# The second half of the last layer down as seven block products over pairs of token tiles

## The chip, the core and the metric

The kernel runs on one core of a Trainium2 chip. The metric is the device time of one execution, in microseconds (us); less is better.

## What is computed

Three stages follow each other: a decayed linear attention, a gated layer pair, and a second layer pair with three branches of which the largest counts. All is float32. The change is in the last line.

```python
# q, k, v: (2, 8, 768, 64), lam: (8,); per block of 64 positions
intra = (q_b @ k_b.T * lam ** (i - j) for i >= j) @ v_b
inter = (q_b * lam ** (i + 1)) @ kv_state
kv_state = lam ** 64 * kv_state + (k_b * lam ** (63 - i)).T @ v_b
x = (intra + inter) as (1536 tokens, 512)
x = ((x @ w_a) * (x @ w_b)) @ w_out                # 512 -> 1536 -> 512
h = max(x @ w1, x @ w2, x @ w3)                    # 512 -> 768
out = h @ w_out                                    # 768 -> 512: the last layer down
```

## The kernel before

**Products in three.** TensorE multiplies a rounded form of float32 (`F32R` in the code). Every operand is split into a high part, a ScalarE copy to that form, and a low part, a VectorE subtraction of the high part from the whole (`split_part`, L525). Each product is then three matmuls: high x high, low x high, high x low.

**Layers up.** All but two column groups of the layers up use Winograd's form of Strassen's product: a 2 x 2 block product in seven block products (`PROD`) with sums of operand blocks before (S1 to S4, T1 to T4) and sums of results after. `Group.product` (L591) issues six matmuls of 384 columns for each; `largest` (L655) adds the results up and keeps the maximum of the three branches in six tiles `m0` to `m5` of 128 features x 1536 tokens each (`ha` in the code). Their first 768 columns are the first half of the tokens.

**The last layer down.** `down2` (L775) multiplies the tokens, 12 tiles of 128, with the 768 x 512 weights; tokens are the stationary operand and the weights stream through. The first half, tiles 0 to 5, goes feature group by feature group (k = 0 to 5) into six PSUM banks, `out0` to `out5`, all open at once: 108 matmuls of 512 columns. The first two of its 36 steps are issued among the last products of the layer up. At k = 5 each tile's bank is copied to SBUF by ScalarE (`ob`) and sent out by a DMA of SP's queue (`store`, L752). The second half, tiles 6 to 11, goes tile by tile: 18 matmuls of 512 columns each, the last tile in two halves of 256 columns, whose last copy is VectorE's (L761). PSUM has eight banks of 512 columns.

**Weights.** They come in as 64-bit numbers and are put together by `converted` (L211): VectorE shifts (L221), ScalarE scales (L224), VectorE merges twice (L229, L231). `down_block` (L310) does this for blocks of 768 columns and splits them: four blocks for the last layer, put in pairs in `dh`, `dl` (k = 0 to 2) and `hd`, `ld` (k = 3 to 5).

**Order.** Each engine has a queue of its own and takes it in the order in which it was written. A planner (`Pace`) writes the work of VectorE and ScalarE between the matmuls: a task is a generator whose steps are written as soon as its gates are open and its engine is estimated to have room (`pump`), or at the latest when somebody needs the result (`need`). The splits of `m0` to `m5` are such tasks, for either half of the tokens (`finished2`, L1021). SBUF work tiles come from a ring of 26 slots of 1536 columns (`slot`), the PSUM banks from a ring of eight (`bank`).

Of the kernel before, what the change touches and what calls it, by code (L numbers as in the profile page):

```python
# [11 lines left out]
F32R = mybir.dt.float32r  # L12
AF = mybir.ActivationFunctionType
ALU = mybir.AluOpType

B, H, S, D = 2, 8, 768, 64
# [3 lines left out]
NT = B * S  # L20
# [5 lines left out]
K2 = F2 // 128  # L26
J = 384
TT = 512
NTT = NT // TT
WB = 768  # L30
ND1 = K1 * DM // WB
ND2 = K2 * DM // WB
N1 = K1
N2 = 3 * K2 // 2
# [9 lines left out]
PROD = {  # L44
    1: ("A11", "B11", "z"), 6: ("S2", "T2", "z"), 7: ("S3", "T3", "z"), 4: ("A22", "T4", "z"),
    2: ("A12", "B21", "x"), 5: ("S1", "T1", "b"), 3: ("S4", "B22", "b"),
}
FIRST = (1, 2, 5)
# [115 lines left out]
def decay_attention_gated_mlps(ctx: ExitStack, tc: tile.TileContext, qkv: bass.AP, lam: bass.AP, wup: bass.AP, wdown: bass.AP, out: bass.AP):  # L164
    nc = tc.nc
# [6 lines left out]
    pace = Pace()  # L172

    def slot(name, dt=F32):
        return sp.tile([128, 1536], dt, tag="s", name=name)

    def zt(name):
        return zp.tile([128, J], F32, tag="z", name=name)

    def bank(name):  # L180
        return pp.tile([128, 512], F32, tag="ps", name=name)

    def rd(t):
        return t.bitcast(F32)

    def tt(e, o, a, b, op):
        (nc.vector if e == "DVE" else nc.gpsimd).tensor_tensor(out=o, in0=a, in1=b, op=op)  # L187

    def copy(o, a):
        nc.scalar.activation(out=o, in_=a, func=AF.Copy)  # L190
# [4 lines left out]
    at_item = {x: n for n, x in enumerate(items)}  # L195
# [110 lines left out]
        tt(e, t7[:, 6], t7[:, 2], t7[:, 0], ALU.subtract)  # L306

    dparts, dunit = {}, {}

    def down_block(m, i):  # L310
        roomy = 1 <= i < ND1 - 1 or i == ND1 + 3
        yield "gate", ("done", m - (2 if roomy or i == ND1 + 1 else 1))
        yield "gate", ("conv", m)
        t = yield from converted(m, WB, roomy)
        yield "gate", ("split", m)
        if i in (0, ND1 + 2):
            dparts[i // 2] = [hp.tile([128, 1536], F32R, tag="h", name=f"{x}{i}", padded_shape=[128, 1792]) for x in ("hd", "ld")]
        elif i % 2 == 0:
            dparts[i // 2] = slot(f"dh{i}", F32R), slot(f"dl{i}", F32R)
        hi, lo = dparts[i // 2]  # L320
        s = slice(WB * (i % 2), WB * (i % 2) + WB)
        yield ("ACT",), WB, "S"
        copy(hi[:, s], t[:, 0:WB])
        e = yield EITHER, WB, "S"
        tt(e, lo[:, s], t[:, 0:WB], rd(hi[:, s]), ALU.subtract)
        pace.open(("done", m))
        for k in range(3):
            if k // 2 <= i % 2 and (i // 2, k) not in dunit and (k == 0 or i % 2):
                dunit[i // 2, k] = hi[:, 512 * k:512 * k + 512], lo[:, 512 * k:512 * k + 512]

# [20 lines left out]

    def unit(first, k):
        b = first // 2 + k // 3
        m = at_item["down", first + (3 * (k // 3) * 512 // WB) + (0 if k % 3 == 0 else 1)]
        items_to(m)
        pace.need(wtask[m], lambda: (b, k % 3) in dunit)
        return dunit[b, k % 3]
# [167 lines left out]
    def split_part(a, h, l):  # L525
        n = a.free_size()
        yield ("ACT",), n, "S"
        copy(h, a)
        e = yield EITHER, n, "S"
        tt(e, l, a, rd(h), ALU.subtract)  # L530

    class Operands:
# [6 lines left out]
        def __init__(self, a, name, order=ORDER, given={}):  # L539
            self.ops, self.name, self.given = dict(given), name, given  # L540
            plain = order is not self.ORDER
            for x in given:
                pace.open((name, "part", x))
            a11, a12, a21, a22 = a[0][:, 0:2], a[0][:, 2:4], a[1][:, 0:2], a[1][:, 2:4]
            s12 = slot(f"{name}s12").rearrange("p (s a n) -> p s a n", s=2, a=2)
            s1, s2 = s12[:, 0], s12[:, 1]
            self.sums = {"S1": (s1, a21, a22, ALU.add), "S2": (s2, s1, a11, ALU.subtract), "S3": (a21, a21, a11, ALU.subtract), "S4": (s1, a12, s2, ALU.subtract)}
            self.src = {"A11": a11, "S1": s1, "S2": s2, "A12": a12, "A21": a21, "S3": a21, "A22": a22, "S4": s1}
            self.tasks = {}
            for i, x in enumerate(order):  # L550
                t = self.tasks[x] = pace.add(self.make(i if not plain else x, x, plain), 0.7 if plain and x[0] == "S" else 0)
                for g in ("sum", "part"):
                    pace.opens[name, g, x] = t
# [30 lines left out]
    class Group:  # L584
# [6 lines left out]
        def product(self, p):  # L591
            a, b, where = PROD[p]
            if p in FIRST:
                self.bank[where] = bank(f"{where}{self.name}")
            ps = self.bank[where][:, 0:J]
            wh, wl = weights(self.n, b)
            xh, xl = self.ops(self.j).get(a)
            todo = [(w[:, 128 * k:128 * k + 128], x[:, k]) for k in range(2) for w, x in ((wh, xh), (wh, xl), (wl, xh))]
            for i, (w, x) in enumerate(todo):
                nc.tensor.matmul(ps, w, x, start=p in FIRST and i == 0, stop=i == len(todo) - 1, skip_group_check=p not in FIRST)  # L600
            pace.pe(6 * MM, self.free.get(where, 0.0))
            if p in (1, 6, 7):
                z = self.z[p] = zt(f"z{p}{self.name}")
                copy(z, ps)
                self.free["z"] = pace.run("ACT", J)
            self.done(self, p, ps)
# [28 lines left out]
    def tokens(j, b):  # L635
        return slice((2 * j + b) * J, (2 * j + b) * J + J)
# [16 lines left out]
    ha = {}  # L653
# [98 lines left out]
    def store(i, c, cols, ps, vector=False):  # L752

        j, b, r = i // 6, i // 3 % 2, i % 3
        row = b * S + j * J + 128 * r
        s = slice(c, c + cols)
        if c == 0:
            store.ob = slot(f"ob{i}")
        ob = store.ob
        if vector:  # L760
            nc.vector.tensor_copy(ob[:, s], ps)  # L761
        else:
            copy(ob[:, s], ps)
            pace.run("ACT", cols)
        nc.sync.dma_start(out=out[row:row + 128, s], in_=ob[:, s])

    def down2_part(i, k, ps, s):
        o = tokens(i // 6, i // 3 % 2).start + 128 * (i % 3)
        (ah, al), (wh, wl) = hs[k], unit(ND1, k)
        pace.need(htask[k, i // 6])  # L770
        for n, (a, w) in enumerate(((ah, wh), (al, wh), (ah, wl))):
            nc.tensor.matmul(ps, a[:, o:o + 128], w[:, s], start=k == 0 and n == 0, stop=k == K2 - 1 and n == 2)  # L772
        pace.pe(3 * MM5 * (s.stop - s.start) / 512)

    def down2():  # L775

        n = NT // 128
        ps = {}
        for k in range(K2):
            for i in range(6):  # L780
                if k == 0:
                    ps[i] = bank(f"out{i}")
                down2_part(i, k, ps[i], slice(0, 512))
                if k == K2 - 1:
                    store(i, 0, 512, ps[i])
                yield
        for i in range(6, n):
            last = i == n - 1
            cols = 256 if last else 512
            for c in range(0, 512, cols):  # L790
                p = bank(f"out{i}_{c}")[:, c:c + cols]
                for k in range(K2):
                    down2_part(i, k, p, slice(c, c + cols))
                store(i, c, cols, p, last and c > 0)

    with tc.manual_schedule():
        nc.sync.dma_start(out=lams, in_=lam)
# [218 lines left out]
            pace.open(("y0", i))  # L1016
            pace.open(("y1", i))
        yo[1] = Operands([ya[1, b] for b in range(B)], "y1")
        hs, htask = {}, {}

        def finished2(at, g):  # L1021
            n = g.n - N1
            f, i = divmod(n, 3)
            if g.j == 1:
                for d in (n + 2, n + 3):
                    if d < N2:
                        open_to("conv", base + d)
                if n + 2 < N2:
                    open_to("split", base + n + 2)
                for d in {N2 - 3: (0,), N2 - 2: (1,), N2 - 1: (2, 3)}.get(n, ()):  # L1030
                    open_to("conv", base + N2 + d)
                    open_to("split", base + N2 + d)
            if i == 2:
                for k in (f, f + K2 // 2):
                    if g.j == 0:
                        hs[k] = slot(f"hh{k}", F32R), slot(f"hl{k}", F32R)
                    s = slice(768 * g.j, 768 * g.j + 768)
                    htask[k, g.j] = pace.add(split_part(ha[k][:, s], hs[k][0][:, s], hs[k][1][:, s]), 2)

        def each2(at, g):  # L1040
            f, i = divmod(g.n - N1, 3)
# [7 lines left out]
        for i, _ in enumerate(in_slots(groups, each2, finished2)):  # L1049
            if 7 * len(groups) - i in (3, 2):  # L1050
                next(then)
        for _ in then:
            pass

# [50 lines left out]
```

## Time and profile before

| | |
|---|---|
| median of 3 runs | 508.27 us (508.13 to 508.62) |
| the profiled execution | 508.21 us |
| its span from first to last instruction | 506.5 us |
| TensorE matmuls, busy | 499.0 us (99%) |
| VectorE, busy | 376.9 us (74%) |
| ScalarE, busy | 213.6 us (42%) |
| GpSimd, busy | 57.7 us (11%) |

Busy time is the time in which an engine has an instruction under way. Matmuls overlap in the records, so their distance, not their length, tells how fast TensorE goes. PE is TensorE's matmul, PEld its weight load, DVE VectorE, ACT ScalarE, POOL GpSimd, SP the engine whose queue issues the DMAs.

### The profile page before, as it was taken

How to read it: one execution, taken by the hardware profiler on the slowest of the kernel's cores; microseconds unless marked ns; L12 is line 12 of the kernel's file. 1: busy time of each engine (PE TensorE's matmuls, PEld its weight loads, DVE VectorE, ACT ScalarE, POOL GpSimd, SP SyncE). 2: the span in 40 equal slices, each digit the busy share in tenths (PEclk: the TensorE clock that was granted, in tenths of full speed). 3: DMA queues.
4: the chain of work that ended last, by engine and by line, in shares of the span. 5: the costliest groups of instructions: out<-in, count | busy, mean ns of one | idle time of the engine just before them, and what ended most of it. 6: DMA issues, size and time to landing. Idle time of an engine off the chain costs nothing.

```text
span 506.5 us, 7757 instructions
## 1 busy us (share of the span) xinstructions
PE 499.0 (99%) x3163; PEld 466.2 (92%) x3163; DVE 376.9 (74%) x559; ACT 213.6 (42%) x360; POOL 57.7 (11%) x50
## 2 busy tenths in 40 slices
PE   7899999999999999999999999999999999999997
PEld 6799899999999999997888888899999999998886
DVE  6899878787788777789685089679998999897000
ACT  2434445343344443445542455543554454433211
POOL 4685200211111011211000000000000000000000
PEclk9999999999999999999999999999999999999999
DMA  8996002222222101314331021102211111110311
GB/s 295 412 410 257 2 1 84 83 84 83 84 83 85 59 11 58 125 63 129 142 107 60 0 83 32 54 1 83 84 60 47 63 62 63 63 63 0 126 62 63
DMA packets 10404, 47.17 MB, mean 93 GB/s; under 512 B 1280, under 2 KB 1536, under 8 KB 7808
## 3 DMA queue, kind: packets, MB, share of 16 engines
q1 hardware_dynamic: 10368, 46.67, 25.1%
q8 instruction: 25, 0.41, 0.3%
q14 instruction: 11, 0.09, 0.1%
HBM read 43.52 MB, written 3.15 MB: 92 GB/s over the span
## 4 chain that ended last, share of the span: by engine, by line
PE 94%; DVE 4%; DMA 1%; issue 0%; ACT 0%; SPq 0%; DVEq 0%
PE yp L718 18%; PE zu L600 16%; PE zv L600 15%; PE out L772 10%; PE bu L600 8%; PE bv L600 7%; PE p L619 7%; PE xu L600 4%; PE xv L600 4%; PE s L416 2%; PE o L472 1%; DVE am L423 1%; PE k L485 1%; PE o L459 1%; DMA aq<-qkv_dram 1%; DVE gl L187 1%
## 5 line engine op out<-in xcount | busy, mean ns | idle before, releaser
L187 DVE TENSOR_TENSOR lo<-w,hi 128x1024 fp32r<-128x1024 f32 (+2 forms) x41 | 48.2, 1175 | 12.4 <-ACT hi L190 12.4
L190 ACT ACTIVATE hi<-w 128x1024 fp32r<-128x1024 f32 (+2 forms) x41 | 38.5, 938 | 22.7 <-DVE w L262 6.9
L718 PE MATMUL yp<-gh,dh 128*128 128x512 f32 x108 | 42.0, 389 | 0.0
L718 PE MATMUL yp<-gl,dh 128*128 128x512 f32 x108 | 42.0, 389 | 0.0
L718 PE MATMUL yp<-gh,dl 128*128 128x512 f32 x108 | 42.0, 389 | 0.0
L650 POOL TENSOR_TENSOR g<-z1u,z6u 128x384 f32<-128x384 f32 x20 | 24.0, 1199 | 149.9 <-DVE z6u L632 149.9
L187 DVE TENSOR_TENSOR gl<-g,gh 128x512 fp32r<-128x512 f32 x36 | 24.7, 707 | 17.8 <-ACT gh L190 17.8
L187 DVE TENSOR_TENSOR w<-w 128x256 f32<-128x256 f32 (+1 forms) x57 | 30.9, 541 | 1.0
L761 DVE COPY ob<-out 128x256 f32<-128x256 f32 x1 | 0.4, 425 | 38.4 <-PE out L772 38.4
L229 DVE SCALAR_TENSOR_TENSOR w<-ws,w 128x1024 int32<-128x1024 int32 x20 | 26.0, 1300 | 1.1 <-ACT ws L224 1.1
L231 DVE SCALAR_TENSOR_TENSOR w<-ws,w 128x1024 int32<-128x1024 int32 x20 | 25.8, 1288 | 0.3
L190 ACT ACTIVATE z6u<-zu 128x384 f32<-128x384 f32 x20 | 9.8, 492 | 38.2 <-PE zu L600 38.1
L190 ACT ACTIVATE z7u<-zu 128x384 f32<-128x384 f32 x20 | 9.8, 492 | 34.3 <-PE zu L600 34.3
L718 PEld LDWEIGHTS yp<-gh,dh 128*128 128x128 f32 x108 | 20.3, 188 | 4.2
L718 PEld LDWEIGHTS yp<-gl,dh 128*128 128x128 f32 x108 | 20.3, 188 | 4.2
L190 ACT ACTIVATE gh<-g 128x512 fp32r<-128x512 f32 x36 | 21.1, 620 | 7.2 <-PE yp L718 7.2
L718 PEld LDWEIGHTS yp<-gh,dl 128*128 128x128 f32 x108 | 20.3, 188 | 4.2
L224 ACT ACTIVATE ws<-wr 128x1024 f32<-128x1024 f32 x20 | 23.0, 1151 | 1.3 <-DMA wr<-wup_dram 1.3
L600 PE MATMUL zu<-x1A,hi 128*128 128x384 f32 x80 | 20.3, 334 | 0.0
L600 PE MATMUL bu<-x0S,hi 128*128 128x384 f32 x80 | 20.3, 334 | 0.0
L600 PE MATMUL bu<-x1S,hi 128*128 128x384 f32 x80 | 20.3, 334 | 0.0
L600 PE MATMUL zu<-x1S,hi 128*128 128x384 f32 x80 | 20.3, 334 | 0.0
(205 smaller groups left out, 1441.9 us busy)
## 6 DMA issues: line engine op xcount, KB each, us to landing
wr<-wup_dram SPq DMA_DIRECT2D x20, 1024.0 KB, 4.8
wr<-wdown_dram SPq DMA_DIRECT2D x12, 768.0 KB, 4.3
aq<-qkv_dram SPq DMA_DIRECT2D x12, 512.0 KB, 11.4
av<-qkv_dram SPq DMA_DIRECT2D x10, 512.0 KB, 10.8
out_dram<-ob SPq DMA_DIRECT2D x11, 256.0 KB, 2.0
wr<-wup_dram SPq DMA_DIRECT2D x2, 512.0 KB, 10.3
av<-qkv_dram SPq DMA_DIRECT2D x2, 256.0 KB, 9.9
out_dram<-ob SPq DMA_DIRECT2D x2, 128.0 KB, 1.7
```

Of the source, the lines that this page charges most:

```text
L187: (nc.vector if e == "DVE" else nc.gpsimd).tensor_tensor(out=o, in0=a, in1=b, op=op)
L190: nc.scalar.activation(out=o, in_=a, func=AF.Copy)
L224: nc.scalar.activation(out=near, in_=high.bitcast(F32), func=AF.Copy, scale=2.0 ** -112)
L229: nc.vector.scalar_tensor_tensor(out=w, in0=near, scalar=3, in1=w, op0=ALU.logical_shift_left, op1=ALU.bitwise_or)
L231: nc.vector.scalar_tensor_tensor(out=w, in0=near, scalar=-0x80000000, in1=w, op0=ALU.bitwise_and, op1=ALU.bitwise_or)
L416: nc.tensor.matmul(sc[n][i][:, o], k[rows(i), o], q[rows(i), o], start=True, stop=True)
L423: nc.vector.tensor_tensor(out=am[n][:, 512 * i:512 * i + 512], in0=sc[n][i], in1=decay[:, 4 * i:4 * i + 4].rearrange("p a i -> p (a i)"), ...
L600: nc.tensor.matmul(ps, w, x, start=p in FIRST and i == 0, stop=i == len(todo) - 1, skip_group_check=p not in FIRST)
L619: nc.tensor.matmul(ps, w[:, 128 * k:128 * k + 128], x[:, k], start=m == 0, stop=m == 11)
L650: nc.gpsimd.tensor_tensor(out=ga[g.n][:, tokens(g.j, 0)], in0=g.z[1], in1=g.z[6], op=ALU.mult)
L718: nc.tensor.matmul(ps[e], w[:, cols], g, start=k == 0 and m == 0, stop=k == K1 - 1 and m == 2)
L772: nc.tensor.matmul(ps, a[:, o:o + 128], w[:, s], start=k == 0 and n == 0, stop=k == K2 - 1 and n == 2)
```

## The change

**Products.** The second half of the tokens is taken as a 2 x 2 block product too. The row blocks are the two batches (384 tokens each, three tiles), the inner blocks features 0 to 383 and 384 to 767, the column blocks the two halves of 256 output columns. A `Tile` (r = 0, 1, 2) is a pair of token tiles, one of each batch; each of its seven products is nine matmuls of 256 columns. `ORDER2` goes product by product (1, 2, 5, 6, 7, 4, 3), the three pairs in turn. A pair holds three banks: `zo` for products 1, 6, 7, 4, `xo` for 2, `bo` for 5 and 3. Results are added by VectorE (`Tile.sum`) or copied by ScalarE into `ob`.

**Operands.** `operands2` makes the four sums of token blocks and the four of weight blocks in place, and the splits of all seven token operands and four weight sums, as one stretch of VectorE and ScalarE instructions. It is written when the last product of the layer up has been written, after what is left of the first half's splits and of the four weight blocks (`finish`), and before what is left of the first half's matmuls and copies. The planner has no say in it. The splits of the second half that the layer up had among its work (six copies and six subtractions of 768 elements) are gone.

**Weights.** The four blocks now hold one quarter of the matrix each (the host puts them so), and their parts are written with a stride, so that `dh`, `hd` still hold 512 columns for each k. A pair of blocks must be whole before any of its three k is used. The high and low parts of the first half's features f and f + 3 share a slot.

```diff
 def down_block(m, i):
+    late = i >= ND1
...
+    w = t[:, 0:WB]
+    if late:
+        h, l = (x.rearrange("p (k t n) -> p k t n", k=3, t=2)[:, :, i % 2] for x in (hi, lo))
+        w = w.rearrange("p (k n) -> p k n", k=3)
...
-    for k in range(3):
+    if late:
+        dwide[i - ND1] = t[:, 0:WB]
+    for k in range(0 if not late or i % 2 else 3, 3):
...
 def down2():
...
-    for i in range(6, n):
-        last = i == n - 1
-        cols = 256 if last else 512
-        for c in range(0, 512, cols):
-            p = bank(f"out{i}_{c}")[:, c:c + cols]
-            for k in range(K2):
-                down2_part(i, k, p, slice(c, c + cols))
-            store(i, c, cols, p, last and c > 0)
+    tiles = [Tile(r) for r in range(3)]
+    for r, p in ORDER2:
+        tiles[r].product(p)
+
+ORDER2 = [(r, p) for p in (1, 2, 5, 6, 7, 4, 3) for r in range(3)]
+
+class Tile:
...
+    def product(self, p):
+        r = self.r
+        a, b, where = PROD[p]
...
+        if p in FIRST:
+            self.bank[where] = bank(f"{where}o{r}")
+        ps = self.bank[where][:, 0:256]
+        n = 0
+        for f in range(K2 // 2):
+            (wh, wl), (ah, al) = quarter(b, f), parts[f, a]
+            for x, w in ((ah, wh), (al, wh), (ah, wl)):
+                nc.tensor.matmul(ps, x[:, 128 * r:128 * r + 128], w, start=p in FIRST and n == 0, stop=n == 8, skip_group_check=p not in FIRST)
+                n += 1
...
+        if p in (1, 6, 7):
+            z = self.z[p] = zt(f"z{p}o{r}")[:, 0:256]
+            copy(z, ps)
...
+        if p == 2:
+            self.sum(self.put(0, 0), ps, self.z[1])
+        elif p == 7:
+            self.sum(self.put(1, 1), self.bank["b"][:, 0:256], self.z[7])
...
+        elif p == 4:
+            copy(self.put(1, 0), ps)
...
+            self.send(1)
+        elif p == 3:
+            if r == 2:
+                self.send(0, 0)
+            self.sum(self.put(0, 1), ps, self.z[6])
+            self.send(0, 1 if r == 2 else None)
...
+def operands2():
...
+    for n, x in enumerate(("A22", "A11", "A12", "S1", "T1", "S3", "T3", "S2", "T2", "S4", "T4")):
+        todo = []
+        if x[0] == "T":
+            o, a, b = (w[v] for v in tinto[x])
+            tt("DVE", o, a, b, ALU.subtract)
...
+            todo.append((o, *dsum[x]))
+        else:
+            for f in range(K2 // 2):
+                if x in into:
...
+                    tt("DVE", o, a, b, op)
...
+                todo.append((blocks[f, x], *parts[f, x]))
+        for a, h, l in todo:
+            copy(h, a)
...
+        for a, h, l in later:
+            tt("DVE", l, a, rd(h), ALU.subtract)
...
+        later = todo
...
 def finished2(at, g):
...
     if i == 2:
-        for k in (f, f + K2 // 2):
-            if g.j == 0:
-                hs[k] = slot(f"hh{k}", F32R), slot(f"hl{k}", F32R)
-            s = slice(768 * g.j, 768 * g.j + 768)
-            htask[k, g.j] = pace.add(split_part(ha[k][:, s], hs[k][0][:, s], hs[k][1][:, s]), 2)
+        if g.j == 1:
+            return
+        both = slot(f"hh{f}", F32R), slot(f"hl{f}", F32R)
+        for i, k in enumerate((f, f + K2 // 2)):
+            hs[k] = tuple(x[:, 768 * i:768 * i + 768] for x in both)
+            htask[k, 0] = pace.add(split_part(ha[k][:, 0:768], *hs[k]), 2)
...
     for i, _ in enumerate(in_slots(groups, each2, finished2)):
         if 7 * len(groups) - i in (3, 2):
             next(then)
+    for k in range(K2):
+        finish(htask[k, 0])
+    for d in range(4):
+        finish(wtask[base + N2 + d])
+    operands2()
     for _ in then:
         pass
```

The order that comes of it stands here at two places. The first is ScalarE's queue around the six copies that empty the first half's banks (`ob0` and on; `hd` is the second weight pair's high part; `hh` a split of the features). Before:

```order
L190 ACTIVATE z7v81_4207<-zv81_4143 128x384 [waits PE_49]
L190 ACTIVATE hh2_4185<-m2_3808 128x768 [waits DVE_49]
L190 ACTIVATE hh5_4187<-m5_3809 128x768 [waits DVE_49]
L224 ACTIVATE w31_4239<-wr31_4042 128x768 [waits DMAHW1_49]
L224 ACTIVATE wd32_4247<-wr32_4128 128x768 [waits DMAHW2_49]
L190 ACTIVATE hd10_4265<-w31_4239 128x768 [waits DVE_49]
L190 ACTIVATE hd10_4265<-wd32_4247 128x768 [waits DVE_49]
L190 ACTIVATE ob0_4346<-out0_4211 128x512 [waits PE_49]
L190 ACTIVATE ob1_4352<-out1_4223 128x512 [waits PE_49]
```

In the change (`q` are high parts of token operands, `dT1` to `dT4` those of the weight sums):

```order
L190 ACTIVATE dT2_4300<-wd32_4230 128x768 [waits DVE_49,PE_49]
L190 ACTIVATE q010_4274<-m3_3011 128x384 [waits DVE_49]
L190 ACTIVATE q110_4277<-m4_3400 128x384 [waits DVE_49]
L190 ACTIVATE q210_4280<-m5_3801 128x384 [waits DVE_49]
L190 ACTIVATE dT4_4313<-w31_4221 128x768 [waits DVE_49,PE_49]
L190 ACTIVATE ob0_4410<-out0_4197 128x512 [waits PE_49,Activation_49]
L190 ACTIVATE ob1_4416<-out1_4209 128x512 [waits Activation_49]
L190 ACTIVATE ob2_4422<-out2_4319 128x512 [waits Activation_49]
```

The bank copies now stand behind 25 high parts of `operands2`, the last of them that of T4, which waits for VectorE. The second place is TensorE's queue where the second half begins. Before, tile 5's last matmuls and tile 6's first:

```order
L772 MATMUL out5_4255<-hd10_4265,hh5_4187 128x512
L772 MATMUL out5_4255<-hd10_4265,hl5_4188 128x512
L772 MATMUL out5_4255<-ld10_4266,hh5_4187 128x512
L772 MATMUL out6_0_4379<-dh8_4054,hh0_3375 128x512
L772 MATMUL out6_0_4379<-dh8_4054,hl0_3376 128x512
L772 MATMUL out6_0_4379<-dl8_4055,hh0_3375 128x512
```

In the change, the end of the second pair's first product and the start of the third's, 18 matmuls further on than the rows above:

```order
L836 MATMUL zo1_4457<-dh8_4042,q200_4241 128x256
L836 MATMUL zo1_4457<-dh8_4042,q201_4242 128x256
L836 MATMUL zo1_4457<-dl8_4043,q200_4241 128x256
L836 MATMUL zo2_4470<-dh8_4042,q000_4237 128x256 [waits Activation_49]
L836 MATMUL zo2_4470<-dh8_4042,q001_4238 128x256
L836 MATMUL zo2_4470<-dl8_4043,q000_4237 128x256
```

Before, nothing stands between the halves. Now the third pair's first product waits for ScalarE: six banks are the first half's, `zo0` and `zo1` have the other two, and `zo2` takes the bank that `out0` had.

## Rows read from the trace of the kernel before

**Rows 1.** The chain that ended last, from 429 us (start us, us, what).

```profile
455.59 47.89 PE out L772 x228
503.48 0.02 issue
503.50 0.42 DVE ob L761
```

**Rows 2.** Busy time of the engines in stretches of 5 us.

```profile
core 0: us, PE busy (x) PEld busy (x) DVE busy (x) ACT busy (x) POOL busy (x), PEclk, DMA share, GB/s
...
465.00:470.00 5.00, 5.00 (x24) 4.14 (x23) 0.07 (x1) 0.00 (x0) 0.00 (x0) 1.00 0.02 3
470.00:475.00 5.00, 5.00 (x24) 4.14 (x23) 0.00 (x0) 0.00 (x0) 0.00 (x0) 1.00 0.00 0
```

**Rows 3.** TensorE's timeline in the last layer down (start us, us, what).

```profile
451.76 0.39 PE L772 MATMUL out<-dh,hh 128*128 128x512 f32 x1
...
478.59 0.39 PE L772 MATMUL out<-dh,hh 128*128 128x512 f32 x1
...
498.99 0.28 PE L772 MATMUL out<-dh,hh 128*128 128x256 f32 x1
...
503.19 0.28 PE L772 MATMUL out<-ld,hh 128*128 128x256 f32 x1
```

**Rows 4.** VectorE's timeline at the end of the layer up.

```profile
443.67 0.55 DVE L221 TENSOR_SCALAR w<-wr 128x768 int32<-128x768 int32 x1
444.32 0.96 DVE L229 SCALAR_TENSOR_TENSOR w<-w 128x768 int32<-128x768 int32 x1
...
445.79 0.56 DVE L661 TENSOR_TENSOR m<-z1v,m 128x384 f32<-128x384 f32 x1
446.26 0.55 DVE L632 TENSOR_TENSOR z7v<-bv,z7v 128x384 f32<-128x384 f32 x1
...
449.19 0.96 DVE L187 TENSOR_TENSOR dl<-w,dh 128x768 fp32r<-128x768 f32 x1 [0.45 <-ACT dh L190]
...
456.70 0.55 DVE L221 TENSOR_SCALAR w<-wr 128x768 int32<-128x768 int32 x1
...
457.64 0.95 DVE L187 TENSOR_TENSOR hl<-m,hh 128x768 fp32r<-128x768 f32 x1
458.51 0.95 DVE L229 SCALAR_TENSOR_TENSOR w<-w 128x768 int32<-128x768 int32 x1
459.50 0.96 DVE L231 SCALAR_TENSOR_TENSOR w<-w 128x768 int32<-128x768 int32 x1
```

**Rows 5.** ScalarE's timeline in the same stretch and after.

```profile
449.06 0.47 ACT L190 ACTIVATE z6v<-zv 128x384 f32<-128x384 f32 x1
449.43 0.84 ACT L190 ACTIVATE hh<-m 128x768 fp32r<-128x768 f32 x1
...
460.49 0.85 ACT L190 ACTIVATE hd<-w 128x768 fp32r<-128x768 f32 x1 [1.21 <-DVE w L231]
...
475.39 4.00 ACT L190 ACTIVATE ob<-out 128x512 f32<-128x512 f32 x6 [11.31 <-PE out L772]
482.87 0.60 ACT L190 ACTIVATE ob<-out 128x512 f32<-128x512 f32 x1 [3.48 <-PE out L772]
```

**Rows 6.** TensorE's timeline at the start of the span.

```profile
2.35 2.31 PE L815 MATMUL warm_ps<-stt 128*128 128x512 bf16 x5 [2.35 <-ACT stt L810]
4.84 3.77 PE L416 MATMUL s<-aq 64*128 64x128 f32 x32 [0.17 <-DMA aq<-qkv_dram]
...
11.73 2.06 PE L416 MATMUL s<-aq 64*128 64x128 f32 x32
...
14.75 1.09 PE L472 MATMUL o<-am,av 128*64 128x128 f32 x16
17.07 1.09 PE L472 MATMUL o<-am,av 128*64 128x128 f32 x16 [1.22 <-DMA av<-qkv_dram]
```

**Rows 7.** A stretch of 1 us at the start, columns as in rows 2.

```profile
4.00:5.00 1.00, 0.83 (x4) 0.16 (x2) 1.00 (x4) 0.00 (x0) 0.00 (x0) 1.00 0.99 381
```

More of the change, by code (lines that the diff above doesn't have):

```diff
@@ L308, in decay_attention_gated_mlps, with quarter @@
     dparts, dunit = {}, {}
+    dwide, dsum = {}, {}
+    def quarter(x, f):
+        if x[0] == "T":
+            return tuple(v[:, 256 * f:256 * f + 256] for v in dsum[x])
+        o = 256 * (int(x[2]) - 1)
+        return tuple(v[:, o:o + 256] for v in unit(ND1, 3 * (int(x[1]) - 1) + f))
     def down_block(m, i):
+        late = i >= ND1
         roomy = 1 <= i < ND1 - 1 or i == ND1 + 3
@@ L320, in down_block @@
         hi, lo = dparts[i // 2]
-        s = slice(WB * (i % 2), WB * (i % 2) + WB)
+        w = t[:, 0:WB]
[3 more added lines that the diff above has]
+        else:
+            h, l = (x[:, WB * (i % 2):WB * (i % 2) + WB] for x in (hi, lo))
         yield ("ACT",), WB, "S"
-        copy(hi[:, s], t[:, 0:WB])
+        copy(h, w)
         e = yield EITHER, WB, "S"
-        tt(e, lo[:, s], t[:, 0:WB], rd(hi[:, s]), ALU.subtract)
+        tt(e, l, w, rd(h), ALU.subtract)
         pace.open(("done", m))
-        for k in range(3):
+        if late:
+            dwide[i - ND1] = t[:, 0:WB]
+        for k in range(0 if not late or i % 2 else 3, 3):
             if k // 2 <= i % 2 and (i // 2, k) not in dunit and (k == 0 or i % 2):
@@ L353, in unit @@
         b = first // 2 + k // 3
-        m = at_item["down", first + (3 * (k // 3) * 512 // WB) + (0 if k % 3 == 0 else 1)]
+        m = at_item["down", first + 2 * (k // 3) + (0 if k % 3 == 0 and first == 0 else 1)]
         items_to(m)
@@ L775, in down2 @@
     def down2():
-        n = NT // 128
         ps = {}
@@ L786, in down2 @@
                 yield
-        for i in range(6, n):
-            last = i == n - 1
-            cols = 256 if last else 512
-            for c in range(0, 512, cols):
-                p = bank(f"out{i}_{c}")[:, c:c + cols]
-                for k in range(K2):
-                    down2_part(i, k, p, slice(c, c + cols))
-                store(i, c, cols, p, last and c > 0)
+        tiles = [Tile(r) for r in range(3)]
+        for r, p in ORDER2:
+            tiles[r].product(p)
+    OPERANDS = ("A22", "A11", "A12", "S1", "S3", "S2", "S4")
@@ new lines, in decay_attention_gated_mlps, with __init__, put, send @@
+    ORDER2 = [(r, p) for p in (1, 2, 5, 6, 7, 4, 3) for r in range(3)]
+    class Tile:
+        def __init__(self, r):
+            self.r, self.bank, self.z, self.free = r, {}, {}, {}
+            self.ob = None
+        def put(self, b, half):
+            return self.ob[:, 512 * b + 256 * half:512 * b + 256 * half + 256]
+        def send(self, b, half=None):
+            row = b * S + J + 128 * self.r
+            s = slice(0, 512) if half is None else slice(256 * half, 256 * half + 256)
+            nc.sync.dma_start(out=out[row:row + 128, s], in_=self.ob[:, 512 * b + s.start:512 * b + s.stop])
+        def product(self, p):
+            r = self.r
+            a, b, where = PROD[p]
+            if p == 1:
+                self.ob = slot(f"ob{6 + r}")
+            if p in FIRST:
[7 more added lines that the diff above has]
+                    n += 1
+            pace.pe(9 * 0.12, self.free.get(where, 0.0))
+            if p in (1, 6, 7):
+                z = self.z[p] = zt(f"z{p}o{r}")[:, 0:256]
+                copy(z, ps)
+                self.free["z"] = pace.run("ACT", 256)
+            if p == 2:
+                self.sum(self.put(0, 0), ps, self.z[1])
+            elif p == 7:
+                self.sum(self.put(1, 1), self.bank["b"][:, 0:256], self.z[7])
+                self.free["b"] = pace.t["DVE"]
+            elif p == 4:
+                copy(self.put(1, 0), ps)
+                pace.run("ACT", 256)
+                self.send(1)
[4 more added lines that the diff above has]
+                self.send(0, 1 if r == 2 else None)
+        def sum(self, o, ps, z):
+            nc.vector.tensor_tensor(out=o, in0=ps, in1=z, op=ALU.add)
+            pace.run("DVE", 256)
@@ L1018, in decay_attention_gated_mlps, with finish @@
         yo[1] = Operands([ya[1, b] for b in range(B)], "y1")
-        hs, htask = {}, {}
+        hs, htask, parts = {}, {}, {}
+        def finish(task):
+            while task.next is not None:
+                if task.next[0] == "gate":
+                    task.move(None)
+                else:
+                    task.step(pace)
+            pace.gone(task)
+        def operands2():
+            blocks = {}
+            for f in range(K2 // 2):
+                for u in range(2):
+                    for b in range(B):
+                        blocks[f, f"A{b + 1}{u + 1}"] = ha[f + u * (K2 // 2)][:, tokens(1, b)]
+            into = {"S1": ("A22", "A21", "A22", ALU.add), "S3": ("A21", "A21", "A11", ALU.subtract), "S2": ("A11", "S1", "A11", ALU.subtract), "S4": ("A12", "A12", "S2", ALU.subtract)}
+            w = dict(zip(("B11", "B12", "B21", "B22"), (dwide[i] for i in range(4))))
+            tinto = {"T1": ("B11", "B12", "B11"), "T3": ("B12", "B12", "B22"), "T2": ("B22", "B22", "T1"), "T4": ("B21", "B21", "T2")}
+            packs, later = {}, []
+            for n, x in enumerate(("A22", "A11", "A12", "S1", "T1", "S3", "T3", "S2", "T2", "S4", "T4")):
+                todo = []
+                if x[0] == "T":
+                    o, a, b = (w[v] for v in tinto[x])
+                    tt("DVE", o, a, b, ALU.subtract)
+                    pace.run("DVE", WB, kind="S")
+                    w[x] = o
+                    t = slot(f"d{x}", F32R)
+                    dsum[x] = t[:, 0:WB], t[:, WB:2 * WB]
+                    todo.append((o, *dsum[x]))
+                else:
+                    for f in range(K2 // 2):
+                        if x in into:
+                            o, a, b, op = into[x]
+                            o, a, b = (blocks[f, v] for v in (o, a, b))
+                            tt("DVE", o, a, b, op)
+                            pace.run("DVE", J, kind="S")
+                            blocks[f, x] = o
+                        m, q = divmod(OPERANDS.index(x), 4)
+                        if (f, m) not in packs:
+                            packs[f, m] = [slot(f"q{f}{m}{v}", F32R).rearrange("p (s n) -> p s n", s=4) for v in range(2)]
+                        parts[f, x] = tuple(t[:, q] for t in packs[f, m])
+                        todo.append((blocks[f, x], *parts[f, x]))
+                for a, h, l in todo:
+                    copy(h, a)
+                    pace.run("ACT", a.free_size(), kind="S")
+                for a, h, l in later:
+                    tt("DVE", l, a, rd(h), ALU.subtract)
+                    pace.run("DVE", a.free_size(), kind="S")
+                later = todo
+            for a, h, l in later:
+                tt("DVE", l, a, rd(h), ALU.subtract)
+                pace.run("DVE", a.free_size(), kind="S")
@@ L1092 @@
         blocks(ua[:, 0], ub[:, 0], ua[:, 1], ub[:, 1]), np.stack(third, axis=1).reshape(-1, 128, 1024)])).view(np.int64)
+    last = wm.reshape(2, 3, 128, 2, 256).transpose(0, 3, 2, 1, 4).reshape(4, 128, WB)
     wup[0] = wup[0].reshape(128, 4, 256)[:, [1, 2, 0, 3]].reshape(128, 1024)
-    wdown = np.ascontiguousarray(np.concatenate([down(wo), down(wm)])).view(np.int64)
+    wdown = np.ascontiguousarray(np.concatenate([down(wo), last])).view(np.int64)
     heads = np.concatenate([np.tile(np.arange(H), (128, 1)), np.arange(H).reshape(2, NP).repeat(64, axis=0)], axis=1)
```

## The prediction

> **What bounds the kernel now.** I read the chain that ended last first. Its last stretch is TensorE alone: from 455.59 us on, 228 matmuls of the last layer down take 47.89 us, then one VectorE copy of 0.42 us, then the output's landing to the end of the span at 506.5 us [rows 1]. So here time is worth what TensorE's row is worth. Next, VectorE and ScalarE beside it, by stage: VectorE works 0.07 us between 465 and 470 us and nothing in the 5 us after [rows 2]. Those engines are free while TensorE does the first half of the tokens, and the change puts its new work there. The question is whether that work ends before TensorE needs what it makes, or what stands behind it.
>
> **TensorE's own work.** The first half is unchanged (108 matmuls of 512 columns, six of them among the last groups of the layer up). The second half begins at 478.59 us; the 256-column matmuls of the last tile begin at 498.99 us [rows 3]. Between lie five tiles of 18 matmuls: 20.40 us / 90 = 0.2267 us each. The last begins at 503.19 us, 35 after the first of its kind: 4.20 / 35 = 0.120 us each. Before: 90 x 0.2267 + 36 x 0.120 = 24.72 us. After: 3 pairs x 7 products x 9 matmuls = 189 of 256 columns, 189 x 0.120 = 22.68 us. Saved: **2.04 us**, if nothing waits.
>
> **The new stretch on VectorE.** Durations: two 384-element additions that don't need each other start 0.47 us apart (445.79, 446.26 us); a 768-element one holds VectorE 0.87 us (457.64 to 458.51); an instruction that needs the one ahead starts later, 0.65 us after a shift of 768 (443.67, 444.32) and 0.99 us after a bit merge (458.51, 459.50) [rows 4]. All operands lie in SBUF and are of the types measured.
>
> When it can start: up to 456.70 us VectorE's queue is as before [rows 4]. Then stand two weight blocks of the down layer, now one after the other: shift, merge, merge, the high part on ScalarE (0.85 us, begun at 460.49 us, 0.03 us after the merge of 459.50 us ended [rows 4, 5]), the low part. First block: 456.70, 457.35, 458.34, end 459.30, ScalarE to 460.18, low part at 460.21. Second: 461.08, 461.73, 462.72, end 463.68, ScalarE to 464.56, low part 464.59. TensorE wants that block's high part at 466.47 us (48 matmuls of 0.2267 us after 455.59) and its low part two matmuls later, so the first half isn't held; the cover is over 1 us. The stretch starts at 465.46 us.
>
> What it is: 33 instructions of 384 elements (21 low parts, 12 sums) and 8 of 768 (four T sums, four low parts), 33 x 0.47 + 8 x 0.87 = 22.5 us of VectorE, with 25 ScalarE copies beside it, each far ahead of its low part. Up to and with the last sum, T4, stand 30 of the first and 7 of the second kind: 14.2 + 6.1 = 20.3 us (0.473 and 0.873 unrounded). So T4 ends at 465.46 + 20.3 + 0.1 = **485.85 us**.
>
> **What is queued behind it.** ScalarE's order is the heart: the last high part, of T4, stands ahead of the six copies that empty the first half's PSUM banks. It waits for T4: 485.88 to 486.73 us; ScalarE starts the next instruction about 0.1 us before such a one ends (449.06, 449.43 us against their lengths [rows 5]); the first bank copy runs 486.63 to 487.23 us, 0.60 us as such copies take [rows 5]. Before, the six ran from 475.39 us on [rows 5]. Eight banks, six held by the first half: TensorE can start two products, 18 x 0.120 = 2.16 us after 478.59, that is to 480.75 us. The third takes the first tile's bank and waits to 487.29 us: **6.5 us of standing still**. Later banks come free every 0.6 us or less, a product takes 1.08 us: no second wait. Then 19 products, 171 x 0.120 = 20.52 us, to 507.81 us; before, the last matmul made way at 503.31 us. **+4.50 us**, which already holds the 2.04 us saved.
>
> **The rest, with one answer.** Six splits of the second half go (six 768 copies and subtractions): they lay beside a TensorE that never waited; two of them, as the one at 457.64 us [rows 4], stood among the weight blocks, and their going is in the start above. The first pair of weight blocks must now be whole before the first down step at 451.76 us [rows 3]; its second low part ended at 450.15 us (449.19 + 0.96 [rows 4]) and stands in the same place now: nothing. Twelve ScalarE copies of 256 and nine VectorE sums replace six bank copies: each beside a product of 1.08 us; the last sum takes the place of the last copy, 0.42 us. There are 13 output transfers as before; the first six issue 11 us later, all while TensorE still works, and SP's last one waits for the last sum as it did. Weights load the same bytes.
>
> **TensorE's clock after the stop.** No row shows a stop this long. Below: a gap of 1.22 us at 15.8 us left the clock up, the same 16 matmuls taking 1.09 us on either side [rows 6]: price 0. Above: the engine's first work after standing still. Five warming matmuls of 512 columns take 2.31 us, where 5 x 0.2267 and the last one's tail of 0.16 us (0.39 less 0.2267) make 1.29: 1.0 us too much; then 32 small ones take 3.77 us, the same 32 later 2.06 us: 1.7 us too much [rows 3, 6]. [...] So a return from the low level costs 1.7 to 2.7 us. A stop of 6.5 us is nearer to the 2.35 us idle ahead of the warming matmuls than to 1.22 us, so I take the fall, at the middle, **+2.2 us**. [...]
>
> Sum on the profiled execution: 508.21 + 4.50 + 2.2 = **514.9 us**; the median of the runs shown, 508.27 us, lies 0.06 us above, less than I round.
>
> **Rivals.**
> *The clock stays up.* All of the above without the last term: 512.7 us. For it: the 1.22 us gap. Against it: the slow start.
> *The stretch is hidden, and it is faster.* The place is T4's high part on ScalarE. If it ended by 480.1 us, the first bank copy would be done when the third product asks, and the stop is gone: 508.21 - 2.04 = 506.2 us. That needs the stretch up to T4 in 13.8 us instead of 20.3, a third less per instruction. A shift of 768 elements runs in 0.55 us [rows 4], so VectorE has such a rate; but every two-operand row of float32 takes 0.95 us for 768, so I give it little.
> *It does nothing measurable.* The same place, half way: the stop is 2.0 us and eats what the matmuls save, 508.2 us. It needs T4 some 4.5 us earlier; nothing in the rows is so far off.
> [...]
>
> **How the numbers follow.** Forecast (stop and fall) 0.68; clock stays 0.22; hidden 0.04; nothing 0.02; the low clock longer, or the first half held too, 0.04. The range takes the first two: 512.7 less 0.4 for the stop's error, and 512.7 + 2.7 + 0.9 for a return longer than the start's: 512.3 to 516.3 us, with 0.9 of the chance. Faster by over 0.2% (1 us, about what can be told from no change here) 0.04, same 0.02, slower 0.94.
>
> **What would show it.** Right: TensorE idle in the second half once, after 18 matmuls of it, about 6.5 us, ended by ScalarE's first bank copy, itself ended by T4's copy; VectorE full from 456 to about 488 us; 256-column matmuls 0.120 us apart late, 0.24 us apart at first if the clock fell. Wrong: TensorE without that gap, bank copies near 475 us, or a first half that waits for weights.

## The result, and the profile after

The change makes the kernel **slower**: 514.67 us median (513.9 to 515.01, 4 runs) against 508.36 us of the kernel before beside it, a ratio of 1.0121, 95% interval 1.0109 to 1.0133. The profiled execution took 515.01 us, 6.80 us more than the one before, with a span of 513.3 us.

The page first: TensorE's busy time and its row and the granted clock's in 40 slices.

```profile
PE 499.2 (97%) x3226; PEld 469.8 (92%) x3226; DVE 398.0 (78%) x602; ACT 222.6 (43%) x385; POOL 57.9 (11%) x50
...
PE   8899999999999999999999999999999999999597
...
PEclk9999999999999999999999999999999999999989
```

TensorE has 2 us less to do and still ends later: there is a hole in the third slice from the end, and the clock dips in the slice behind it. The chain that ended last (start us, us, what) says what lies in the hole:

```profile
484.99 0.88 DVE w L187
...
485.99 0.71 issue
486.70 0.59 ACT ob L190
487.33 2.29 PE zo L836 x9
489.62 4.46 PE xo L836 x27
494.07 3.24 PE bo L836 x27
497.31 9.72 PE zo L836 x81
507.03 3.25 PE bo L836 x27
510.31 0.42 DVE ob L859
```

Where [rows 1] had one TensorE stretch to the end, the chain now runs over VectorE's last weight sum (`w` at 484.99 us, T4), ScalarE's split of it (the 0.71 us before 486.70) and the copy of the first bank. The last sum starts at 510.31 us, in [rows 1] at 503.50. TensorE's timeline (the idle time ahead of a row and its releaser in brackets):

```profile
478.67 0.40 PE L836 MATMUL zo<-dh,q 128*128 128x256 f32 x2
...
480.70 0.28 PE L836 MATMUL zo<-dl,q 128*128 128x256 f32 x1
487.33 0.79 PE L836 MATMUL zo<-dh,q 128*128 128x256 f32 x2 [6.35 <-ACT ob L190]
...
488.14 0.63 PE L836 MATMUL zo<-dh,q 128*128 128x256 f32 x2
...
488.78 0.63 PE L836 MATMUL zo<-dh,q 128*128 128x256 f32 x2
...
492.48 0.40 PE L836 MATMUL xo<-hd,q 128*128 128x256 f32 x2
...
492.84 0.40 PE L836 MATMUL xo<-hd,q 128*128 128x256 f32 x2
```

After 18 matmuls of the second half it stands still. Then three matmuls take 0.64 us (488.14 to 488.78), 0.213 us each, and from 492.48 us on 0.36 us, 0.120 each. VectorE and ScalarE in the new stretch, one fence each:

```profile
465.63 2.89 DVE L187 TENSOR_TENSOR q<-m,q 128x384 fp32r<-128x384 f32 x6
...
484.91 0.95 DVE L187 TENSOR_TENSOR w<-w,wd 128x768 f32<-128x768 f32 x1
```

```profile
485.95 0.84 ACT L190 ACTIVATE dT<-w 128x768 fp32r<-128x768 f32 x1 [1.27 <-DVE w L187]
486.70 3.02 ACT L190 ACTIVATE ob<-out 128x512 f32<-128x512 f32 x6
```

The six bank copies of 475.39 us [rows 5] start at 486.70 us. The windows of 2 us, columns as in rows 2, show VectorE full up to 488 us and the clock at half from 486 to 492 us:

```profile
484.00:486.00 2.00, 0.00 (x0) 0.00 (x0) 2.00 (x4) 0.73 (x3) 0.00 (x0) 0.87 0.00 0
486.00:488.00 2.00, 0.67 (x3) 0.67 (x4) 2.00 (x4) 2.00 (x4) 0.00 (x0) 0.50 0.00 0
488.00:490.00 2.00, 2.00 (x11) 2.00 (x11) 0.13 (x1) 2.00 (x6) 0.00 (x0) 0.50 0.94 351
490.00:492.00 2.00, 2.00 (x12) 2.00 (x11) 0.37 (x1) 0.55 (x2) 0.00 (x0) 0.50 1.02 381
492.00:494.00 2.00, 2.00 (x17) 2.00 (x17) 0.48 (x2) 0.00 (x0) 0.00 (x0) 0.93 0.15 54
```

Before the change VectorE did nothing between 485 and 490 us, and the clock read 1.00:

```profile
485.00:490.00 5.00, 5.00 (x24) 4.14 (x23) 0.00 (x0) 0.60 (x1) 0.00 (x0) 1.00 0.15 55
```

The trace leaves open whether the place in ScalarE's queue alone makes the stop, and whether the slow matmuls behind it are the clock's or those of the bank copies and output transfers, which run in the same microseconds (DMA share 0.94 and 1.02).

### The profile page after: what moved, and what is told of

Its sections match the earlier page's. It is cut to its first block, busy times and chain, and to the rows that moved or that the text cites. A ratio compares the mean times of both kernels' runs of the same rounds, so it can differ in the third digit from the quotient of the medians.

```text
span 513.3 us, 7965 instructions
## 1 busy us (share of the span) xinstructions
PE 499.2 (97%) x3226; PEld 469.8 (92%) x3226; DVE 398.0 (78%) x602; ACT 222.6 (43%) x385; POOL 57.9 (11%) x50
## 4 chain that ended last, share of the span: by engine, by line
PE 88%; DVE 9%; issue 1%; DMA 1%; ACT 1%; SPq 0%; DVEq 0%; ACTq 0%
PE yp L734 18%; PE zu L616 16%; PE zv L616 15%; PE bu L616 8%; PE bv L616 7%; PE p L635 7%; PE xu L616 4%; PE xv L616 4%; PE zo L836 2%; PE s L432 2%; DVE q L187 2%; PE o L488 1%; PE bo L836 1%; DVE am L439 1%; DVE m L187 1%; PE xo L836 1%
## 5 line engine op out<-in xcount | busy, mean ns | idle before, releaser
L734 PEld LDWEIGHTS yp<-gh,dl 128*128 128x128 f32 x108 | 20.3, 188 | 4.2
L734 PEld LDWEIGHTS yp<-gh,dh 128*128 128x128 f32 x108 | 20.3, 188 | 4.2
L734 PEld LDWEIGHTS yp<-gl,dh 128*128 128x128 f32 x108 | 20.3, 188 | 4.2
L648 DVE TENSOR_TENSOR z6u<-bu,z6u 128x384 f32<-128x384 f32 x20 | 11.1, 552 | 12.2 <-PE bu L616 12.2
L616 PE MATMUL zu<-x1A,hi 128*128 128x384 f32 x80 | 20.3, 334 | 0.0
L616 PE MATMUL zu<-x1S,hi 128*128 128x384 f32 x80 | 20.3, 334 | 0.0
L616 PE MATMUL bu<-x0S,hi 128*128 128x384 f32 x80 | 20.3, 334 | 0.0
L616 PE MATMUL bu<-x1S,hi 128*128 128x384 f32 x80 | 20.3, 334 | 0.0
```

What stands on the lines that cost most here:

```text
L648: nc.vector.tensor_tensor(out=o, in0=ps, in1=z, op=ALU.add)
L734: nc.tensor.matmul(ps[e], w[:, cols], g, start=k == 0 and m == 0, stop=k == K1 - 1 and m == 2)
```

## The experiments

Ratios are to the kernel before beside them: 508.76 us in experiments 1, 2, 5 and 7, 508.67 in 4 and 6, 508.09 (one execution) in 3. The kernel before itself ranged from 508.13 to 509.74 us (15 runs) in the first of these sets and from 508.06 to 509.68 us in the second, so a single execution can't tell a difference of about 1 us. Two readings recur: the row where TensorE starts again, with the stop ahead of it, and the time from there to the last VectorE sum, in which 171 matmuls lie.

**1. The bank copies ahead of T4.** `operands2` is made a generator that yields behind each operand, and the 34 steps left of the first half are written ahead of the last one.

```diff
-operands2()
+made = operands2()
+for _ in range(10):
+    next(made)
+for _ in range(34):
+    next(then)
+for _ in made:
+    pass
```

> The six copies that empty the first half's banks are written one operand earlier, before T4's high part instead of behind it; all VectorE work, every sum and every product stays. Theory (the stop is the copies' place on ScalarE's queue, and the clock falls some 4.5 us after TensorE stopped, as in the changed kernel's trace): the first copy follows S4's last high part, which ended at 484.67 us, so TensorE goes on at about 485.3 instead of 487.33 us: 2.05 us off the stop, 4.3 us left. With the clock up, 508.36 + 2.5 = 510.8 us; if it just falls, up to 513. Rival A (TensorE waits for the sums themselves, or for VectorE's length, wherever ScalarE's copies stand): no shorter stop, 514.7 us.

Measured: **512.43 us** (512.23 to 512.82), ratio 1.0074 (1.0061 to 1.0088). TensorE's restart, and two windows:

```profile
485.30 0.50 PE L836 MATMUL zo<-dh,q 128*128 128x256 f32 x2 [4.24 <-ACT ob L190]
```

```profile
486.00:488.00 2.00, 2.00 (x11) 2.00 (x11) 1.35 (x3) 2.00 (x5) 0.00 (x0) 0.50 0.96 357
488.00:490.00 2.00, 2.00 (x14) 2.00 (x13) 1.29 (x2) 1.24 (x4) 0.00 (x0) 0.69 1.03 384
```

The order on ScalarE alone moves the restart by 2.03 us. The clock still falls, but comes back sooner: the last sum starts at 507.61 us, 2.70 us earlier than with the change, 0.67 of it from the clock.

**2. The bank copies ahead of S4.** The same edit with 9 in place of 10: S4's and T4's splits stand behind the copies.

> The same six copies two operands earlier, behind T2's high part (it ended at 482.24 us) and before S4's and T4's. Theory: first copy 482.2 to 482.8 us, TensorE stops for 2.0 us (480.83 to 482.85), too short for the clock to fall, and the stop eats what the matmuls save: 508.4 us, give or take 0.4, the same as before the change. Rival A: 514.7 us still. Rival B (the slow matmuls after the stop come from the copies and transfers that run beside them, not from the clock): the stop is shorter by 4.5 us but the 2.3 us stay, 510.2 us.

Measured: median **510.02 us**, ratio 1.0016 (1.0002 to 1.003), but in two groups: four of ten runs from 508.24 to 508.73 us, six from 509.72 to 510.75. The profiled execution, 508.24 us, is of the lower group: the stop is 1.81 us, the clock reads 1.00 in all windows behind it, and the last sum starts at 503.51 us, in [rows 1] at 503.50.

```profile
482.71 0.50 PE L836 MATMUL zo<-dh,q 128*128 128x256 f32 x2 [1.81 <-ACT ob L190]
```

The profiled execution is as the theory had it; the median is nearer to the rival's. The mean granted clock listed for each run points to why: 0.996 or 0.997 in all six of the upper group, 1.000 in three of the four others (0.997 in the fourth, at 508.73 us). Experiments 3 and 4 test that reading.

**3. The same kernel, one more execution.**

> The same kernel as copies_before_S4 once more, for a look at an execution of its upper group, if this is one. Theory: where the time is 509.7 us or more, TensorE stops as long as before (1.8 us, to about 482.7 us), the granted clock is at half behind the stop for some microseconds, and the rows from 482.7 us on end about 2 us later than 503.51 us; where the time is under 508.8 us, the clock stays at 1.00. Rival (the upper group waits elsewhere): the extra 2 us lie in another idle time or in an earlier stage, at full clock.

Measured: 509.93 us, an execution of the upper group. TensorE's restart, and three windows:

```profile
482.90 0.50 PE L836 MATMUL zo<-dh,q 128*128 128x256 f32 x2 [1.80 <-ACT ob L190]
...
483.36 0.63 PE L836 MATMUL zo<-dh,q 128*128 128x256 f32 x2
```

```profile
482.00:484.00 2.00, 1.09 (x6) 1.10 (x7) 2.00 (x5) 1.94 (x5) 0.00 (x0) 0.84 0.14 51
484.00:486.00 2.00, 2.00 (x11) 2.00 (x11) 1.98 (x3) 1.81 (x4) 0.00 (x0) 0.50 1.03 381
486.00:488.00 2.00, 2.00 (x16) 2.00 (x16) 1.74 (x4) 2.00 (x6) 0.00 (x0) 0.81 0.95 353
```

The stop is as long as in experiment 2, 1.80 us, everything starts 0.19 us later, and the clock falls this time. The last sum starts at 505.20 us, 1.69 us later than there: the 0.19 and 1.50 us of the clock.

**4. The same kernel with 16 more matmuls in the short stop.** They go behind the second pair's first product, into the unused half of its bank (the results of these 16 are not used).

```diff
+            if (r, p) == (1, 1):
+                for _ in range(16):
+                    nc.tensor.matmul(self.bank[where][:, 256:512], ..., start=False, stop=False, skip_group_check=True)
```

> The kernel with the bank copies ahead of S4, whose times fell in two groups (508.2 to 508.7 and 509.7 to 510.8), with 16 more 256-column matmuls (1.92 us) into an unused half of a PSUM bank in the stop of 1.81 us. Theory (the upper group are executions whose clock fell in that short stop): the fillers add nearly no time and the upper group goes: all runs 508.2 to 508.9. Rival (the upper group comes from elsewhere, from DMA or from another wait): both groups stay, median near 510.

Measured: **508.51 us** (508.04 to 508.9, 11 runs), ratio 0.9996 (0.9987 to 1.0005). The upper group is gone. TensorE, with the added matmuls on L840:

```profile
481.43 2.08 PE L840 MATMUL zo<-dh,q 128*128 128x256 f32 x16
483.39 0.50 PE L836 MATMUL zo<-dh,q 128*128 128x256 f32 x2
```

The windows of 2 us behind it, up to 496 us, all read a clock of 1.00. The last sum starts at 504.19 us, 0.68 us later than in experiment 2, but the second half had begun 0.69 us later too (479.28 us for 478.59). With more matmuls the median is 1.5 us lower, and nothing else in the program was changed. The two sets ran on different chips, so the times alone don't exclude that the chip made the difference; but the windows of experiment 3 show the fall itself, and it cost 1.50 us there. Together they make the upper group of experiment 2 the clock after a stop.

**5. 48 more matmuls in the stop of the change.** The same edit on the changed kernel with 48, so that TensorE works through most of the 6.35 us.

> The changed kernel with 48 further matmuls of 256 columns at the end of the second pair's first product, into the unused half of its bank, which nobody reads: 48 x 0.120 = 5.76 us of work inside the 6.5 us stop; nothing else moves. Theory: the stop's end is ScalarE's, so it stays at 487.3 us, and TensorE has not stood still for long, so the clock stays up: 2.3 us less, 512.4 us, and matmuls 0.120 us apart from the restart on. Rival B (the slow matmuls come from the bank copies and six output transfers beside them): 514.7 us, slow matmuls as before. If the added work itself came late: more than 514.7.

Measured: **513.62 us** (513.55 to 514.29), ratio 1.0101 (1.0086 to 1.0117). TensorE, and the window in which the transfers begin:

```profile
481.24 5.92 PE L840 MATMUL zo<-dh,q 128*128 128x256 f32 x48
487.76 0.51 PE L836 MATMUL zo<-dh,q 128*128 128x256 f32 x2 [0.60 <-ACT ob L190]
...
488.22 0.40 PE L836 MATMUL zo<-dh,q 128*128 128x256 f32 x2
488.57 0.40 PE L836 MATMUL zo<-dh,q 128*128 128x256 f32 x2
```

```profile
488.00:490.00 2.00, 2.00 (x18) 2.00 (x18) 0.55 (x1) 2.00 (x6) 0.00 (x0) 1.00 0.72 268
490.00:492.00 2.00, 2.00 (x19) 2.00 (x18) 0.85 (x2) 0.97 (x4) 0.00 (x0) 1.00 1.05 385
```

The same bank copies and the same transfers (share 0.72 and 1.05) stand beside matmuls 0.117 us apart (0.35 us for three, 488.22 to 488.57) at a granted clock of 1.00, where the change had 0.213 at 0.50. So neither slowed TensorE here: the slow stretch is the clock's. The 171 matmuls win back 2.17 us, as the theory had it. The whole is 1.2 us above its 512.4 us all the same: in this execution the work was 0.4 us late long before the stop (VectorE's `dl` of 439.30 us in the changed kernel starts at 439.69), and the kernel before beside it is 0.4 us slower than it was beside the change. These may be one and the same 0.4 us, so 0.4 to 0.8 us are left, which were not followed up.

**6. The four T sums on GpSimd.** They are taken out of VectorE's row; nothing else moves.

```diff
-tt("DVE", o, a, b, ALU.subtract)
+tt("POOL", o, a, b, ALU.subtract)
```

> The four 768-element T sums go to GpSimd, nothing else moves. Theory (the stop is as long as VectorE's row up to the last operand): VectorE's row is 4 x 0.87 = 3.5 us shorter, of which three sums lie ahead of S4's last sum (484.12 us in the changed kernel), so that ends at 481.5; ScalarE's S4 copies end 0.55 us behind it, T4's high part 0.75 us later, the first bank copy 0.6 us behind that: TensorE restarts near 483.4 us instead of 487.33, a stop of about 2.4 us. A 768-element sum on GpSimd took 1.8 us at the start of the program, so it is no late producer. Time about 514.7 - 3.9 = 510.7 with the clock falling as it did, about 508.5 with the clock up; after a stop so near to 1.8 us either may come. Rival A (VectorE is held while GpSimd works on float32 beside it, each by about as long as the sum takes there): nothing is won, restart at 487 us or later, 514 to 518 us. Rival B (the bank copies wait for something else than the operands): 514.7.

Measured: **517.05 us** (516.6 to 517.54), ratio 1.0167 (1.0154 to 1.0181). My theory fell and rival A came. GpSimd's timeline and VectorE's:

```profile
465.48 1.85 POOL L187 TENSOR_TENSOR w<-w,wd 128x768 f32<-128x768 f32 x1 [14.60 <-DVE wd L231]
468.29 2.03 POOL L187 TENSOR_TENSOR wd<-wd,w 128x768 f32<-128x768 f32 x1 [0.96 <-DVE ld L187]
470.40 2.04 POOL L187 TENSOR_TENSOR w<-w,wd 128x768 f32<-128x768 f32 x1
```

```profile
466.22 1.92 DVE L187 TENSOR_TENSOR ld<-wd,hd 128x768 fp32r<-128x768 f32 x1 [0.91 <-ACT hd L190]
468.07 6.19 DVE L187 TENSOR_TENSOR q<-m,q 128x384 fp32r<-128x384 f32 x6
474.19 1.48 DVE L187 TENSOR_TENSOR m<-m,m 128x384 f32<-128x384 f32 x3
```

The low part `ld` takes 1.92 us instead of 0.96, six token low parts 6.19 instead of 2.89. From `ld` to the three sums behind them lie 7.97 us, with the change 3.69: 4.28 us lost beside 5.92 us of GpSimd, of which 0.74 us lay ahead of `ld`. The first weight pair's low part is as long (1.92 us, at 449.78 us), beside a GpSimd sum of 1.84 us that starts at 449.04 us. The second half begins 1.52 us later than with the change (480.19 us for 478.67); 0.50 us of it had arisen before that low part, and its extra 0.96 us would be most of the rest. What VectorE saves, three sums of 0.87 ahead of S4, is real: from those three sums on, S4's last sum ends 13.1 us later, with the change 15.7. But it is less than what was lost: the bank copies start at 488.45 us instead of 486.70. The trace shows the longer instructions beside GpSimd's; what makes them longer it does not show.

**7. The stretch in three pieces.** The operands up to S3; then what is left of the first half, with its bank copies; then those up to T2; then nine products (1, 2 and 5); then S4 and T4. The low parts of each piece are written before it is left, products yield one by one, and three of the first half's output tiles share a slot.

```diff
-operands2()
+made = operands2()
+next(made)
+for _ in range(34):
+    next(then)
+next(made)
+for _ in range(9):
+    next(then)
+next(made)
...
-        if c == 0:
+        if i % 3 == 0:
             store.ob = slot(f"ob{i}")
-        ob = store.ob
+        ob = store.ob[:, 512 * (i % 3):512 * (i % 3) + 512]
```

> Everything of the change, written in another order: the operands up to S3 and their low parts; then the rest of the first half with its bank copies; then T3, S2, T2 and their low parts; then the products 1, 2 and 5; then S4 and T4; then the other products. The six output tiles of the first half share two SBUF slots. Theory: each engine then reaches everything before TensorE wants it (first copy at about 475.5 us as before the change; S2 and T2 whole at some 484.5 us, wanted at 488.4; T4 at some 490.5, wanted at 494.9), no stop, and the 2.04 us that the matmuls save are left: 508.36 - 2.0 = 506.3 us. Rival A: VectorE has the same 22.5 us of work, so TensorE still waits: 510 us or more.

Measured: **506.52 us** (506.37 to 506.64), ratio 0.9957 (0.9945 to 0.997): faster than either kernel. ScalarE's timeline and the chain that ended last:

```profile
475.61 3.98 ACT L190 ACTIVATE ob<-out 128x512 f32<-128x512 f32 x6
```

```profile
455.79 23.16 PE out L788 x102
478.96 3.23 PE zo L837 x27
...
498.39 3.25 PE bo L837 x27
...
501.66 0.42 DVE ob L860
```

The bank copies are back at 475.61 us [rows 5], between 455.79 us and the last sum the chain has no other engine than TensorE again, the clock reads 1.00 throughout. The last sum starts 1.84 us before that of [rows 1], although the second half began 0.20 us later (478.79 us; [rows 3]: 478.59): 2.04 us, the matmul saving of the prediction to the hundredth. Which of the parts of this edit could be left out was not tried.

## Why the prediction was right, point by point

The readings of the profiled executions together; "between" is the time from the restart to the last sum, in which the same 171 matmuls lie:

| | stop | restart, us | last sum starts, us | between, us |
|---|---|---|---|---|
| the change | 6.35 | 487.33 | 510.31 | 22.98 |
| 1, ahead of T4 | 4.24 | 485.30 | 507.61 | 22.31 |
| 2, ahead of S4, lower group | 1.81 | 482.71 | 503.51 | 20.80 |
| 3, the same, upper group | 1.80 | 482.90 | 505.20 | 22.30 |
| 4, short stop filled | none | 483.39 | 504.19 | 20.80 |
| 5, long stop filled | 0.60 | 487.76 | 508.57 | 20.81 |

- **Matmuls saved, 2.04 us**: shown by experiment 7, where nothing waits.
- **VectorE's stretch, T4 at 485.85 us**: it began 0.17 us later than worked out (465.63 for 465.46) and took 20.2 us for 20.3; T4 ended at 485.86.
- **The queue behind it**: T4's split at 485.95 (485.88 forecast), first bank copy at 486.70 (486.63), restart at 487.33 (487.29). Experiments 1 and 2 show that it is ScalarE's order: moving the copies past one operand or two moves the restart by 2.03 and 4.62 us. From the last matmul's making way (480.82) the stop is 6.5 us, as forecast.
- **What the stop costs without the clock, +4.50 us**: the last sum is 6.81 us later than in [rows 1]; less 2.18 for the clock that is 4.63. Of the 0.13 too much, 0.08 had arisen before the second half began (478.67 us for 478.59).
- **The clock, +2.2 us from between 1.7 and 2.7**: 22.98 less 20.80, **2.18 us**. Experiment 5 shows that it is the clock. No run shows what the bounds were read from, a return of the clock at the start of the span: beside the slow matmuls there [rows 6] the granted clock reads 1.00 [rows 7]. What the runs show in its place is a fall to 0.50 and a return behind the stop. So it is in part luck that the middle of the bounds came out, and after the shorter stops of experiments 1 and 3 a fall and return cost 1.51 and 1.50 us (22.31 and 22.30 less 20.80), under the lower bound of 1.7. The rival in which the clock stays up is what experiment 5 makes, though its 513.62 us are 0.9 us above that rival's 512.7.
- **Costs set at nothing**: the first half wasn't held (its end moved by 0.08 us), and no second stop came. The last transfers wait for the last sum as before.
- **Wrong in a size that didn't enter the sum**: I expected 0.24 us between matmuls at the low clock, twice 0.120, and no run shows that. The rows show 0.213 at a granted clock of 0.50. Had the clock stayed there to the end, 171 x 0.093 = 15.9 us would have come on top of 512.7, 528.6 us in all (an estimate from these rows).
- **Too low a view of what could be had**: the rival "hidden", 506.2 us, asked for a faster VectorE. The same VectorE suffices in the order of experiment 7 (506.52 us). As a forecast for this change it was still rightly small.

## What to carry to other kernels

When new work is put behind a stage, look at what already stands behind that place in each in-order queue: here six short copies behind one late split kept six of the eight PSUM banks occupied and TensorE, when it had filled the other two, waiting; the cure was to write the operands in the order in which the products need them, with the old work between. A stop of the engine that bounds the kernel cost its own length here and, where the clock fell, 1.50 to 2.18 us behind it; 1.8 us was a lottery, so close a gap wholly rather than shorten it. Before moving two-operand float32 work from VectorE to GpSimd, count what VectorE loses beside it, here 4.28 us beside 5.92 us of GpSimd.

## What the runs showed of the hardware that I had not expected

- **A short stop was enough, sometimes.** After 6.35 and 4.24 us the clock fell to 0.50 in the profiled executions, and every run of those two kernels lists a mean of 0.997 or less. After 1.8 us it fell in one profiled execution (0.50 from 484 to 486 us) and stayed up in another. The 1.22 us gap of [rows 6] had left it up (16 matmuls in 1.09 us on either side).
- **The fall can come after the restart.** In experiment 3 the first three matmuls behind the stop take 0.46 us (482.90 to 483.36), as long as in experiment 5 at a clock of 1.00 (487.76 to 488.22), and those from 483.36 us on are 0.213 us apart. After the change it came before it: the window from 484 to 486 us reads 0.87, with TensorE idle.
- **A fall and return cost 1.50 or 1.51 us in experiments 3 and 1, 2.18 us in the change.** At a granted clock of 0.50 a matmul of 256 columns took 0.213 us, at 1.00 0.120: less than twice as long. At the start of the span the granted clock had read 1.00 beside slow matmuls [rows 7]; here, column and spacing change together.
- **VectorE's two-operand float32 instructions took longer beside GpSimd's sums**: 1.92 us instead of 0.96, 6.19 instead of 2.89. About 0.8 us were lost for each microsecond in which both had work (an estimate: 4.28 us lost beside 5.92 - 0.74 = 5.18).
